# Attention output with the values stationary, two heads on two column halves, transposed by where it is written

## The chip, the cores and the metric

The kernel runs on one core of one Trainium2 chip. A core has five engines that work at the same time and wait for each other through semaphores: TensorE (matrix products, PE in the profile; its weight loads are PEld), VectorE (DVE), ScalarE (ACT), GpSimd (POOL) and SyncE (SP, whose queue issues most DMAs here). TensorE reads SBUF and writes PSUM; VectorE and ScalarE bring results from PSUM to SBUF. The metric is the device time of one execution in microseconds. All data are fp32.

## What is computed

The first part is a gated linear recurrence for 4 batches and 8 heads over 768 steps with head size 48. The second part is a layer with an oscillating activation on the 3072 x 384 result.

```python
for t in range(S):                                   # S = 768
    new_re = ar * S_re - ai * S_im                   # complex gate a[t], kept below magnitude 0.999
    new_im = ar * S_im + ai * S_re
    kv = np.einsum('bhd,bhe->bhde', k[:, :, t], v[:, :, t])
    S_re, S_im = (new_re + kv, new_im)
    y[:, :, t] = np.einsum('bhd,bhde->bhe', q[:, :, t], S_re)
...
x = y.transpose(0, 2, 1, 3).reshape(B * S, H * D)    # 3072 x 384
h = x @ w_in                                         # 384 x 2048
out = (h * np.cos(h)) @ w_out                        # 2048 x 384
```

## The kernel before

The kernel has a path for ordinary inputs (`fast_path`) and a general one that is taken only if a flag says that the products of gates have become too small; the profiled inputs take the first.

**Tiling.** Time is cut into chunks of C = 128 steps, 6 for each batch, N = 24 in all. G = 2 chunks make a group, so there are NG = 12 groups. The recurrence is turned into matrix products per chunk: the queries and the keys of each head are multiplied by running products of gates and stacked (real and imaginary part, 2 x 48 = 96 rows), so that the chunk's output is a masked 128 x 128 matrix of scores times the chunk's values, plus the queries times a 96 x 48 state that comes from the chunks before.

**Stages of a group**, and the lines that matter here:

- gates (`g_log`, `g_prod`, `g_angle`, `g_phase`, `g_trig`, `g_stack`): ScalarE, VectorE and GpSimd work out logarithms, angles and running products; TensorE sums over time with triangular matrices (`lgs` L662, `phs` L697 and L700).
- chunks, for each of the two chunks: `f_transpose` (TensorE transposes the keys and queries of four heads at a time into `tp`, L734, ScalarE copies them to `kT` and `qT`, L736); `f_scores` (`sc`, L744, masked by VectorE into `atm`, L746, which holds for each head the scores transposed, keys on the partitions and queries along the free dimension); `f_state` (`sp`, L769, the new state by VectorE and GpSimd, not for the last chunk of a batch); `f_out`; `f_xt`.
- `f_out` (L749 to L761): for each head, the scores `atm` are the stationary operand and the 48 columns of the values move (L755); where a state exists, the queries `qT` are stationary and the state's 48 columns move (L758), added in PSUM. The result `yp` has the 128 steps on the partitions and 8 x 48 columns. One ScalarE copy brings it to the SBUF tile `x` (L761). There is no state for the first chunk of a batch.
- `f_xt` (L782 to L789): the layer needs `x` with its 384 columns on the partitions, so TensorE transposes three blocks of 128 x 128 into `xp` (L788) and ScalarE copies them to `xT` (L789), a tile with 3 blocks for the two chunks of a group.
- `mm1` (L791 to L808), eight times a group: 2 x 3 products with blocks of `w_in` stationary and 256 moving columns of `xT` (`hp`, L796), then ScalarE (L802, and the sine at L619), VectorE (L803, L805, L807) make the gate.
- `mm2` (L810 to L817), twice a group: 16 products into `op` (L813), a ScalarE copy to `ot` (L816) and the store, issued on SP's queue (L817).

**Order.** The loop at L851 runs over `it`; at each `it` the gates of group `it`, the chunks of group `it - 1`, the `mm1` of group `it - 2` and the `mm2` of group `it - 3` are in work. `mm2` is written first, and the rest is interleaved by position (`weave`, L841). [...] `load` (L541) brings `re`, `im`, `k`, `q`, `v` by DMAs on SP's queue; the load of `v` for the group after the next is written behind the chunks of a group (L838). The weights are loaded and converted from 64-bit floats in the first pass of the loop.

PSUM has two rings of buffers: `pa` (5) for everything but the layer, `pm` (3) for `hp` and `op`. The pool `ft` holds two buffers of each of its tiles.

Of the kernel before, what the change touches and what calls it, by code (L numbers as in the profile page):

```python
# [11 lines left out]
F32 = mybir.dt.float32  # L12
# [473 lines left out]
def fast_path(ctx, tc, q, k, v, a_re, a_im, moe_w_in, moe_w_out, out, least):  # L486
# [4 lines left out]
    nc = tc.nc  # L491
    B, H, S, D = q.shape
    DM, DF = moe_w_in.shape
    C = 128
    NCH = S // C
    G = 2
# [3 lines left out]
    HH = H // 2  # L500
    ND = DM // C
# [7 lines left out]
    ft = ctx.enter_context(tc.tile_pool(name="ft", bufs=2))  # L509
    msb = ctx.enter_context(tc.tile_pool(name="msb", bufs=2))  # L510
    stage = ctx.enter_context(tc.tile_pool(name="stage", bufs=2))
    rows_d = ctx.enter_context(tc.tile_pool(name="rows_d", bufs=2, space=bass.MemoryType.DRAM))
    pa = ctx.enter_context(tc.tile_pool(name="pa", bufs=5, space=PSUM))
# [7 lines left out]
    def constant(array, name):  # L521
        t = consts.tile(list(array.shape), F32, name=name)
        nc.scalar.dma_start(out=t, in_=nc.inline_tensor(array, name=name + "_const").ap())
        return t
# [6 lines left out]
    X = [dict() for _ in range(NG)]  # L531
    Y = [dict() for _ in range(N)]

    def load(g, names):
        for name in names:
            ap = {"re": a_re, "im": a_im, "q": q, "k": k, "v": v}[name]
            X[g][name] = ld.tile([C, G, H, D], F32, tag=name, name=name,
                                 bufs=2 if name == "v" else 1)
            for i in range(G):
                b, c = divmod(g * G + i, NCH)  # L540
                nc.sync.dma_start(  # L541
                    out=X[g][name][:, i],
                    in_=ap[b].rearrange("h (c p) d -> p c h d", p=C)[:, c])
# [3 lines left out]
    ident = constant(np.eye(C, dtype=np.float32), "ident")  # L547
# [27 lines left out]
    def from_double(dst, src):  # L575
# [24 lines left out]
        nc.vector.scalar_tensor_tensor(out=dst, in0=e, scalar=897.0, in1=dst,  # L600
                                       op0=ALU.is_ge, op1=ALU.mult)

    chained = []

    def chain(ins):
# [121 lines left out]
    def f_transpose(n, name, hh):  # L727
        g, i = divmod(n, G)
        if hh == 0:
            Y[n][name] = ft.tile([D2, H, C], F32, tag=name, name=name)  # L730
        ps = pa.tile([D2, HH, C], F32, tag="a", name="tp")
        for h in range(HH):
            head = i * H + hh * HH + h
            nc.tensor.transpose(ps[:, h], X[g][name[0] + "s"][:, head].rearrange(  # L734
                "p a d -> p (a d)"), ident)
        nc.scalar.copy(out=Y[n][name][:, ts(hh, HH)], in_=ps)  # L736

    def f_scores(n, hh):
        y = Y[n]
        if hh == 0:  # L740
            y["atm"] = ft.tile([C, H, C], F32, tag="atm", name="atm")
        ps = pa.tile([C, HH, C], F32, tag="a", name="sc")
        for h in range(HH):
            nc.tensor.matmul(ps[:, h], lhsT=y["kT"][:, hh * HH + h], rhs=y["qT"][:, hh * HH + h],  # L744
                             start=True, stop=True)
        nc.vector.tensor_tensor(out=y["atm"][:, ts(hh, HH)], in0=ps,  # L746
                                in1=causal.unsqueeze(1).to_broadcast([C, HH, C]), op=ALU.mult)

    def f_out(n):  # L749
        y, (g, i) = Y[n], divmod(n, G)  # L750
        vals = X[g]["v"][:, i]
        state = y.get("state")
        ps = pa.tile([C, H, D], F32, tag="a", name="yp")
        for h in range(H):
            nc.tensor.matmul(ps[:, h], lhsT=y["atm"][:, h], rhs=vals[:, h],  # L755
                             start=True, stop=(state is None))
            if state is not None:
                nc.tensor.matmul(ps[:, h], lhsT=y["qT"][:, h], rhs=state[:, h],  # L758
                                 start=False, stop=True)
        y["x"] = ft.tile([C, DM], F32, tag="x", name="x")  # L760
        nc.scalar.copy(out=y["x"], in_=ps.rearrange("p h d -> p (h d)"))  # L761

    def f_state(n):
        if n % NCH == NCH - 1:
            return
        y, (g, i) = Y[n], divmod(n, G)
        ps = pa.tile([D2, H, D], F32, tag="a", name="sp")
        for h in range(H):
            nc.tensor.matmul(ps[:, h], lhsT=X[g]["ks"][:, i * H + h].rearrange("p a d -> p (a d)"),  # L769
                             rhs=X[g]["v"][:, i, h], start=True, stop=True)  # L770
        new = ft.tile([D2, H, D], F32, tag="state", name="state")
        end = X[g]["end"][:, ts(i, H)].unsqueeze(2).to_broadcast([D2, H, D])
        if "state" in y:
            nc.vector.scalar_tensor_tensor(out=new, in0=ps, scalar=0.25, in1=y["state"],  # L774
                                           op0=ALU.mult, op1=ALU.add)
            nc.gpsimd.tensor_tensor(out=new, in0=new, in1=end, op=ALU.mult)  # L776
        else:
            nc.vector.scalar_tensor_tensor(out=new, in0=ps, scalar=0.25, in1=end,
                                           op0=ALU.mult, op1=ALU.mult)
        Y[n + 1]["state"] = new  # L780

    def f_xt(n):  # L782
        g, i = divmod(n, G)
        if i == 0:
            X[g]["xT"] = msb.tile([C, ND, G, C], F32, tag="xT", name="xT")
        ps = pa.tile([C, ND, C], F32, tag="a", name="xp")
        for dc in range(ND):
            nc.tensor.transpose(ps[:, dc], Y[n]["x"][:, ts(dc, C)], ident)  # L788
        nc.scalar.copy(out=X[g]["xT"][:, :, i], in_=ps)  # L789

    def mm1(g, jp):  # L791
        x = X[g]
# [34 lines left out]
    def chunks(g):  # L827
        ns = range(g * G, g * G + G)
        for n in ns:
            for name in ("kT", "qT"):  # L830
                for hh in range(2):
                    yield lambda n=n, name=name, hh=hh: f_transpose(n, name, hh)
            for hh in range(2):
                yield lambda n=n, hh=hh: f_scores(n, hh)
            yield lambda n=n: f_state(n)
            yield lambda n=n: f_out(n)
            yield lambda n=n: f_xt(n)
        if g + 2 < NG:  # L838
            yield lambda: load(g + 2, ("v",))

# [10 lines left out]
    for it in range(NG + 3):  # L851
        g, c, m, o = it, it - 1, it - 2, it - 3
        if it == 0 and NG > 1:
            load(1, ("v",))
        if g < NG:
            g_log(g)
            g_prod(g)
            g_angle(g)
            if g + 1 < NG:
                load(g + 1, ("re", "im"))  # L860
        if it == 0:
            weave((gates(0), 0.0, 1.0), (weights, 0.2, 1.0))
            continue
        if 0 <= o < NG:
            for i in range(G):
                mm2(o, i)
        weave((gates(g) if g < NG else (), 0.0, 0.5),
              (chunks(c) if 0 <= c < NG else (), 0.0, 1.0),
              ([lambda jp=jp: mm1(m, jp) for jp in range(NJ // 2)] if 0 <= m < NG else (),
               0.0, 1.0))  # L870


@with_exitstack
def kernel(ctx, tc, q, k, v, a_re, a_im, moe_w_in, moe_w_out, out):

    nc = tc.nc
    D2, H = 2 * q.shape[3], q.shape[1]
    keep = ctx.enter_context(tc.tile_pool(name="keep", bufs=1))  # L880
    least = keep.tile([D2, 2 * H], F32, name="least")
    fast_path(tc, q, k, v, a_re, a_im, moe_w_in, moe_w_out, out, least)
    low = keep.tile([D2, 1], F32, name="low")
    nc.vector.tensor_reduce(out=low, in_=least, axis=AX.X, op=ALU.min)
    scratch = ctx.enter_context(tc.tile_pool(name="scratch", bufs=1,
                                             space=bass.MemoryType.DRAM))
    line_d = scratch.tile([D2], F32, name="line_d")
    nc.sync.dma_start(out=line_d, in_=low.rearrange("p o -> (p o)"))
    line = keep.tile([1, D2], F32, name="line")
    nc.sync.dma_start(out=line, in_=line_d.unsqueeze(0))  # L890
    bad = keep.tile([1, 2], F32, name="bad")
    nc.vector.tensor_reduce(out=bad[:, 0:1], in_=line, axis=AX.X, op=ALU.min)
    flag = keep.tile([1, 1], I32, name="flag")
    nc.vector.tensor_scalar(out=flag, in0=bad[:, 0:1], scalar1=0.5, scalar2=None, op0=ALU.is_lt)
    taken = nc.values_load(flag[0:1, 0:1], min_val=0, max_val=1,
                           skip_runtime_bounds_check_because="a comparison gives 0 or 1")
    with tc.If(taken > 0):
        general_path(tc, q, k, v, a_re, a_im, moe_w_in, moe_w_out, out)
# [30 lines left out]
```

## Time and profile before

| | us |
|---|---|
| median of 3 runs | 931.01 |
| lowest and highest | 930.38, 933.06 |
| the profiled execution | 938.23 |
| its span, first to last instruction | 936.4 |

Busy time by engine over the span is TensorE 797.1 us, VectorE 497.1, ScalarE 378.6, GpSimd 171.3. The largest groups of matmuls:

```profile
L796 PE MATMUL hp<-xT,w_in 128*128 128x256 f32 x1152 | 294.0, 409 | 4.1 <-DVE gate L807 3.5
L813 PE MATMUL op<-w_out,gate 128*128 128x384 f32 x768 | 251.1, 486 | 0.0
L744 PE MATMUL sc<-qT,kT 96*128 96x128 f32 x384 | 48.4, 277 | 0.1
```

How to read such a row: line, engine, operation, the tile written and the tiles read; then `128*128`, the rows and columns of the stationary operand, and `128x256`, the partitions and columns of the moving one; the count; then busy time in all and the mean duration in ns of one instruction; then the engine's idle time ahead of them and who ended it. Durations of matmuls overlap each other, so that the time a run of them takes is read from start to start, not by adding durations. Windows name a stretch of the span, its length, the busy time of an engine with its number of instructions, and the clock that TensorE was granted as a share of full speed.

### The profile page before, as it was taken

The page shows a single profiled execution, that of the slowest core. Times are in us where ns is not written, and L with a number is a line of the kernel's source. Part 1 is how long each engine was busy: PE and PEld are TensorE (multiplying, and loading weights), DVE is VectorE, ACT ScalarE, POOL GpSimd, SP SyncE. Part 2 cuts the span into 40 slices and gives each one's busy share as a digit, 9 for nine tenths or more (in the row PEclk, how much of TensorE's full clock was granted, in tenths as well). Part 3 has the DMA queues.
Part 4 walks back from the last instruction along what each step waited for, and adds up shares of the span by engine and source line. Part 5 has one row for each costly group of instructions (what it writes and reads, how often), then busy time and mean ns, then how long its engine had stood idle before and what let it go on. Part 6 is the DMA issues. An engine that isn't in the chain of part 4 may idle for free.

```text
span 936.4 us, 10169 instructions
## 1 busy us (share of the span) xinstructions
PE 797.1 (85%) x3920; PEld 621.0 (66%) x3920; DVE 497.1 (53%) x761; ACT 378.6 (40%) x588; POOL 171.3 (18%) x96
## 2 busy tenths in 40 slices
PE   1101446899999999999999999999999989999997
PEld 0000245685885977967968858858769668778684
DVE  3999985844544736636545446346456445123160
ACT  5222123535454554454364454354544623123140
POOL 2343333403103022112120031031030211000000
PEclk9999966899899999989899999898999998998999
DMA  8523631303004004004023040040040100000000
GB/s 174 141 90 112 146 108 34 69 18 63 23 18 85 1 18 85 1 17 85 1 43 60 18 83 3 18 85 1 18 84 1 26 10 1 9 9 1 9 8 21
DMA packets 151876, 42.03 MB, mean 45 GB/s; under 512 B 144638, under 2 KB 148222, under 8 KB 151818
## 3 DMA queue, kind: packets, MB, share of 16 engines
q1 hardware_dynamic: 151218, 40.98, 19.8%
q8 instruction: 33, 0.54, 0.3%
q10 hardware_dynamic: 600, 0.30, 0.1%
q14 instruction: 25, 0.20, 0.1%
HBM read 36.51 MB, written 4.76 MB: 44 GB/s over the span
## 4 chain that ended last, share of the span: by engine, by line
PE 70%; ACT 6%; DVE 2%; POOL 2%; DMA 1%; issue 1%; ACTq 0%; SPq 0%; POOLq 0%; DVEq 0%
PE hp L796 28%; PE op L813 17%; PE yp L755 4%; PE sc L744 4%; PE yp L758 4%; PE tp L734 4%; PE sp L769 3%; POOL m L646 2%; ACT rs L619 2%; PE lgs L662 1%; ACT L618 1%; PE phs L697 1%; PE phs L700 1%; PE xp L788 1%; ACT m L619 1%; ACT mag L619 1%
## 5 line engine op out<-in xcount | busy, mean ns | idle before, releaser
L796 PE MATMUL hp<-xT,w_in 128*128 128x256 f32 x1152 | 294.0, 409 | 4.1 <-DVE gate L807 3.5
L796 PEld LDWEIGHTS hp<-xT,w_in 128*128 128x128 f32 x1152 | 231.0, 207 | 39.7 <-DVE gate L807 3.9
L813 PE MATMUL op<-w_out,gate 128*128 128x384 f32 x768 | 251.1, 486 | 0.0
L813 PEld LDWEIGHTS op<-w_out,gate 128*128 128x128 f32 x768 | 145.9, 190 | 99.2
L803 DVE TENSOR_SCALAR cs<-turn 128x512 f32<-128x512 f32 x96 | 42.4, 443 | 172.9 <-ACT turn L802 172.9
L802 ACT ACTIVATE turn<-hp,quarter_b 128x512 f32<-128x512 f32 x96 | 65.7, 685 | 124.6 <-PE hp L796 122.7
L807 DVE TENSOR_TENSOR gate<-hp,cs 128x512 f32<-128x512 f32 x96 | 66.2, 690 | 82.2 <-ACT cs L619 81.4
L776 POOL TENSOR_TENSOR state<-state,end 96x384 f32<-96x384 f32 x16 | 31.2, 1949 | 342.2 <-DVE state L774 179.1
L755 PE MATMUL yp<-v,atm 128*128 128x48 f32 x384 | 75.3, 292 | 19.3 <-DVE atm L746 19.3
L619 ACT ACTIVATE cs<-cs 128x512 f32<-128x512 f32 x96 | 60.5, 630 | 69.0 <-DVE cs L805 69.0
L662 PE MATMUL lgs<-m,sums 128*128 128x384 f32 x48 | 21.3, 572 | 64.6 <-POOL m L646 49.3
L755 PEld LDWEIGHTS yp<-v,atm 128*128 128x128 f32 x384 | 62.0, 209 | 20.4 <-DVE atm L746 20.2
L758 PE MATMUL yp<-state,qT 96*128 96x48 f32 x320 | 67.7, 296 | 0.0
L805 DVE TENSOR_TENSOR cs<-turn,cs 128x512 f32<-128x512 f32 x96 | 65.9, 687 | 2.1
L662 PEld LDWEIGHTS lgs<-m,sums 128*128 128x128 f32 x48 | 9.2, 211 | 75.2 <-POOL m L646 71.3
L646 POOL TENSOR_TENSOR m<-m,rs 128x768 f32<-128x768 f32 x12 | 22.0, 1835 | 197.6 <-ACT rs L619 196.7
L697 PE MATMUL phs<-sq,sums 128*128 128x384 f32 x48 | 22.4, 557 | 38.8 <-DVE sq L688 38.8
L758 PEld LDWEIGHTS yp<-state,qT 96*128 96x128 f32 x320 | 54.2, 212 | 0.0
L761 ACT COPY x<-yp 128x384 f32<-128x384 f32 x24 | 11.5, 478 | 104.6 <-PE yp L758 94.0
L633 ACT ACTIVATE m<-re 128x768 f32<-128x768 f32 x12 | 10.1, 842 | 97.3 <-DMA re<-in_a_re_dram 97.3
L744 PE MATMUL sc<-qT,kT 96*128 96x128 f32 x384 | 48.4, 277 | 0.1
L744 PEld LDWEIGHTS sc<-qT,kT 96*128 96x128 f32 x384 | 46.9, 192 | 2.3 <-ACT qT L736 1.0
(77 smaller groups left out, 955.0 us busy)
## 6 DMA issues: line engine op xcount, KB each, us to landing
raw<-in_moe_w_in_dram SPq DMA_DIRECT2D x12, 512.0 KB
raw<-in_moe_w_out_dram SPq DMA_DIRECT2D x16, 384.0 KB
re<-in_a_re_dram SPq DMA_DIRECT2D x24, 192.0 KB
im<-in_a_im_dram SPq DMA_DIRECT2D x24, 192.0 KB
k<-in_k_dram SPq DMA_DIRECT2D x24, 192.0 KB
q<-in_q_dram SPq DMA_DIRECT2D x24, 192.0 KB
v<-in_v_dram SPq DMA_DIRECT2D x24, 192.0 KB
out_dram<-ot SPq DMA_DIRECT2D x24, 192.0 KB
```

The costliest lines, as they stand in the source:

```text
L619: chain(nc.scalar.activation(func=func, **kw))
L646: nc.gpsimd.tensor_tensor(out=m2, in0=m2, in1=rs, op=ALU.subtract)
L662: nc.tensor.matmul(ps, lhsT=sums, rhs=x["lg"][:, ts(i, DM)], start=True, stop=True)
L744: nc.tensor.matmul(ps[:, h], lhsT=y["kT"][:, hh * HH + h], rhs=y["qT"][:, hh * HH + h], start=True, stop=True)
L755: nc.tensor.matmul(ps[:, h], lhsT=y["atm"][:, h], rhs=vals[:, h], start=True, stop=(state is None))
L758: nc.tensor.matmul(ps[:, h], lhsT=y["qT"][:, h], rhs=state[:, h], start=False, stop=True)
L796: nc.tensor.matmul(ps[:, ji], lhsT=w_in[:, dc, ts(jp * 2 + ji, C)], rhs=x["xT"][:, dc].rearrange("p g t -> p (g t)"), start=(dc == 0), sto ...
L802: nc.scalar.activation(out=turn, in_=ps, func=AF.Identity, scale=INV_TWO_PI, bias=quarter_b)
L803: nc.vector.tensor_scalar(out=cs, in0=turn, scalar1=ROUND, scalar2=ROUND, op0=ALU.add, op1=ALU.subtract)
L805: nc.vector.tensor_tensor(out=cs, in0=turn, in1=cs, op=ALU.subtract)
L807: nc.vector.tensor_tensor(out=gate, in0=ps, in1=cs, op=ALU.mult)
L813: nc.tensor.matmul(ps, lhsT=X[g]["gate"][j // 2][:, j % 2, ts(i, C)], rhs=w_out[:, j], start=(j == 0), stop=(j == NJ - 1))
```

## The change

The output of a chunk is computed with the operands exchanged. For each head the 48 columns of the values are stationary and the 128 columns of `atm` move; then the state's 48 columns are stationary and the queries' 128 columns move. What comes out has the head's 48 dimensions on the partitions and the 128 steps along the free dimension: it is already transposed. Heads go in pairs: the even head of a pair is written to partitions 0 to 47 of PSUM, the odd one to partitions 64 to 111, and the pair `p` to columns block `p`. In each pair the order is: values of the even head, values of the odd head, state of the even head, state of the odd head. [...]

Two ScalarE copies per chunk (48 partitions x 512 each, one for each half) bring `yp` to a new tile `yT`, one buffer, which holds both chunks of a group. `f_xt` runs once a group instead of once a chunk. It has no transposes and no copy: DMAs on SP's queue bring the rows of each head from `yT` to their place in `xT`. The 48 rows of a head lie in one block of 128 or in two, so there are 10 DMAs a group, of 48, 32 or 16 partitions with 256 contiguous floats in each. The tile `x` goes. `queries` and the named `keys` in `f_state` change nothing in what is executed.

```diff
     def f_out(n):
         y, (g, i) = Y[n], divmod(n, G)
         vals = X[g]["v"][:, i]
         state = y.get("state")
-        ps = pa.tile([C, H, D], F32, tag="a", name="yp")
-        for h in range(H):
-            nc.tensor.matmul(ps[:, h], lhsT=y["atm"][:, h], rhs=vals[:, h],
-                             start=True, stop=(state is None))
+        if i == 0:
+            X[g]["yT"] = ft.tile([C, HH, G, C], F32, tag="yT", name="yT", bufs=1)
+        ps = pa.tile([C, HH, C], F32, tag="a", name="yp")
+        for p in range(HH):
+            for side in range(2):
+                nc.tensor.matmul(ps[ds(side * 64, D), p], lhsT=vals[:, 2 * p + side],
+                                 rhs=y["atm"][:, 2 * p + side], start=True, stop=(state is None))
             if state is not None:
-                nc.tensor.matmul(ps[:, h], lhsT=y["qT"][:, h], rhs=state[:, h],
-                                 start=False, stop=True)
-        y["x"] = ft.tile([C, DM], F32, tag="x", name="x")
-        nc.scalar.copy(out=y["x"], in_=ps.rearrange("p h d -> p (h d)"))
+                for side in range(2):
+                    nc.tensor.matmul(ps[ds(side * 64, D), p], lhsT=state[:, 2 * p + side],
+                                     rhs=queries(y, 2 * p + side), start=False, stop=True)
+        for side in range(2):
+            half = ds(side * 64, D)
+            nc.scalar.copy(out=X[g]["yT"][half, :, i], in_=ps[half])
...
-    def f_xt(n):
-        g, i = divmod(n, G)
-        if i == 0:
-            X[g]["xT"] = msb.tile([C, ND, G, C], F32, tag="xT", name="xT")
-        ps = pa.tile([C, ND, C], F32, tag="a", name="xp")
-        for dc in range(ND):
-            nc.tensor.transpose(ps[:, dc], Y[n]["x"][:, ts(dc, C)], ident)
-        nc.scalar.copy(out=X[g]["xT"][:, :, i], in_=ps)
+    def f_xt(g):
+
+        xt = X[g]["xT"] = msb.tile([C, ND, G, C], F32, tag="xT", name="xT")
+        for h in range(H):
+            row = h * D
+            while row < (h + 1) * D:
+                n = min((h + 1) * D, (row // C + 1) * C) - row
+                nc.sync.dma_start(out=xt[ds(row % C, n), row // C],
+                                  in_=X[g]["yT"][ds(h % 2 * 64 + row - h * D, n), h // 2])
+                row += n
...
             yield lambda n=n: f_state(n)
             yield lambda n=n: f_out(n)
-            yield lambda n=n: f_xt(n)
+            if n == ns[-1]:
+                yield lambda: f_xt(g)
```

More of the change, by code (lines that the diff above doesn't have):

```diff
@@ L736, in f_transpose, with queries @@
         nc.scalar.copy(out=Y[n][name][:, ts(hh, HH)], in_=ps)
+    def queries(y, h):
+        return y["qT"][:, h]
     def f_scores(n, hh):
@@ L743, in f_scores @@
         for h in range(HH):
-            nc.tensor.matmul(ps[:, h], lhsT=y["kT"][:, hh * HH + h], rhs=y["qT"][:, hh * HH + h],
+            nc.tensor.matmul(ps[:, h], lhsT=y["kT"][:, hh * HH + h], rhs=queries(y, hh * HH + h),
                              start=True, stop=True)
@@ L768, in f_state @@
         for h in range(H):
-            nc.tensor.matmul(ps[:, h], lhsT=X[g]["ks"][:, i * H + h].rearrange("p a d -> p (a d)"),
-                             rhs=X[g]["v"][:, i, h], start=True, stop=True)
+            keys = X[g]["ks"][:, i * H + h].rearrange("p a d -> p (a d)")
+            nc.tensor.matmul(ps[:, h], lhsT=keys, rhs=X[g]["v"][:, i, h], start=True, stop=True)
         new = ft.tile([D2, H, D], F32, tag="state", name="state")
```

## The prediction

> **What bounds the kernel now.** I read the page first (busy times, the clock line, the chain that ended last), then windows over single periods of the main loop, then the timeline of TensorE.
>
> ```profile
> PE 797.1 (85%) x3920; PEld 621.0 (66%) x3920; DVE 497.1 (53%) x761; ACT 378.6 (40%) x588; POOL 171.3 (18%) x96
> PE 70%; ACT 6%; DVE 2%; POOL 2%; DMA 1%; issue 1%; ACTq 0%; SPq 0%; POOLq 0%; DVEq 0%
> ```
>
> TensorE is busy 85% of the span of 936.4 us and holds 70% of the chain; no other engine passes 53%. The view of windows cuts the loop from one `lgs` matmul to the next, which is one group of two chunks (columns: stretch, its length, PE busy and instructions, granted clock, DMA share, GB/s):
>
> ```profile
> 284.54:348.79 64.25, 63.05 (x323) 0.97 0.19 38
> 482.14:544.70 62.56, 61.37 (x323) 1.00 0.20 39
> 199.60:868.40 668.80, 655.55 (x3315) 0.95 0.15 31
> ```
>
> In each period TensorE idles 1.2 us. The two single periods hold the same 323 instructions; the one granted 0.97 of the clock is 1.69 us longer. So in this stretch the time follows TensorE one for one, and TensorE's clock too. Over the 668.8 us from 199.6 to 868.4 the clock averages 0.95. Where it goes is in the timeline of TensorE (start, duration, line, operation, count):
>
> ```profile
> 567.86 1.95 PE L744 MATMUL sc<-qT,kT 96*128 96x128 f32 x16
> 569.64 2.75 PE L796 MATMUL hp<-xT,w_in 128*128 128x256 f32 x12
> 572.24 1.48 PE L769 MATMUL sp<-v,ks 128*96 128x48 f32 x16
> 573.55 0.39 PE L755 MATMUL yp<-v,atm 128*128 128x48 f32 x2
> 573.78 0.39 PE L758 MATMUL yp<-state,qT 96*128 96x48 f32 x2
> ...
> 577.25 4.38 PE L796 MATMUL hp<-xT,w_in 128*128 128x256 f32 x12
> 581.47 0.49 PE L788 MATMUL xp<-ident,x 128*128 128x128 f32 x3
> 581.79 1.04 PE L734 MATMUL tp<-ident,ks 128*96 128x128 f32 x8
> 582.67 2.76 PE L796 MATMUL hp<-xT,w_in 128*128 128x256 f32 x12
> ```
>
> Pitch is read from start to start. Twelve `hp` of 256 moving columns take 2.60 us (569.64 to 572.24), 217 ns each; sixteen `sc` of 128 columns take 1.78, 111 ns each: 0.85 ns a column. But `yp` moves only 48 columns, 41 ns worth, and still needs 112 ns (0.23 to 0.22 us for two, 32 in 3.6 us), and `sp`, also 48 columns, 82 ns (1.31 for 16). 112 to 82 is the ratio of their stationary widths, 128 to 96: these two are held by the weight load, and the array streams 36% and 50% of their time. Right behind them the same twelve `hp` take 4.38 instead of 2.76 us: the clock has halved. Eleven such dips lie between 199.6 and 868.4, the first and last of the view of windows and its sum over all eleven being
>
> ```profile
> 204.96:208.60 3.64, 3.64 (x12) 0.54 0.57 108
> ...
> 843.80:850.60 6.80, 6.80 (x24) 0.54 0.00 1
> sum 59.24, PE 59.24; mean PE 5.39
> ```
>
> All eleven begin inside a `yp` run or at its end, with TensorE busy in its rows. They come only where `sp` and a full `yp` stand together (1.3 + 3.6 = 4.9 us of thin streaming). Behind the shorter stretch of a batch's first chunk (no state, 3.1 us) the clock stays:
>
> ```profile
> 512.00:520.00 8.00, 8.00 (x52) 1.00 0.00 1
> ```
>
> 59.24 us at about half clock are 29 us lost. That the dips are caused by thin streaming is my reading of where they begin; the trace doesn't name a cause.
>
> [...]
>
> **The change part by part.** *The products.* The groups by form:
>
> ```profile
> L755 PE MATMUL yp<-v,atm 128*128 128x48 f32 x384 | 75.3, 292 | 19.3 <-DVE atm L746 19.3
> L758 PE MATMUL yp<-state,qT 96*128 96x48 f32 x320 | 67.7, 296 | 0.0
> L788 PE MATMUL xp<-ident,x 128*128 128x128 f32 x72 | 14.4, 318 | 1.1 <-ACT x L761 1.1
> L761 ACT COPY x<-yp 128x384 f32<-128x384 f32 x24 | 11.5, 478 | 104.6 <-PE yp L758 94.0 <-PE yp L755 10.6
> L789 ACT COPY xT<-xp 128x384 f32<-128x384 f32 x24 | 11.4, 474 | 7.7 <-PE xp L788 7.7
> L736 ACT COPY qT<-tp 96x512 f32<-96x512 f32 x48 | 27.0, 582 | 0.7 <-PE tp L734 0.5
> ```
>
> An fp32 product is two matmul rows (24 chunks x 8 heads = 192 products, 384 rows), and the count stays at 704. Each now holds 48 columns stationary and moves 128: 111 ns by the `sc` row, with a weight load of about 41 ns hidden under it (an estimate from the 82 and 112 ns). Taken singly nothing is won. The even head writes output partitions 0 to 47, the odd one 64 to 111, so the two use separate column halves of the array. No row shows two matmuls at once. Bounds per chunk with state (32 rows): wholly serial, 32 x 0.112 = 3.58 us as now; overlapped, the second row of one half beside the first of the other half, 17 slots of 0.112 = 1.90 us. I take the overlap, since the sides share no stationary columns and no output partitions, and program order alternates them after every product. Entering and leaving the split array may empty the pipeline: a pair of rows lasts 0.39 us while the next starts 0.22 later, a tail of 0.166. Bounds 0 and two tails a chunk; I take two, 0.33 us. So 2.23 us a chunk, 1.35 won; a chunk without state 9 x 0.112 + 0.33 = 1.34 for 1.79, 0.45 won. From chunk 2 on there are 19 and 3 of them: 25.7 + 1.3 = **27 us**.
>
> [...]
>
> *The clock.* The new `yp` streams 128 columns in every slot, so the thin stretch shrinks to `sp`'s 1.3 us, below the 3.1 us that left the clock whole. All eleven dips go: **29 us** (bounds 0 and 29).
>
> *The transposes.* Three `xp` rows take 0.33 us from 581.47 to 581.79 (x72 in all); 22 chunks give **7 us**. The waits for `x` were 1.1 us, nothing.
>
> *ScalarE.* Two copies go (478 and 474 ns), two of 48x512 come; the row of the same 512 elements a partition has 582. That is 0.21 us more a chunk, 5 us in all, behind TensorE: the 94.0 us of idle time before L761 hide it. Uncovered it would cost those 5. Can ScalarE and VectorE follow a faster TensorE? At the end `hp` runs alone and they keep its pace of 2.6 us:
>
> ```profile
> 888.92 20.88 PE L796 MATMUL hp<-xT,w_in 128*128 128x256 f32 x96
> ```
>
> *The ten DMAs a group.* Eight heads, two of them cut at a 128 boundary: 10 DMAs of 16 to 48 partitions, 1 KB a partition, from SP's queue. What stands there now, and the cover on TensorE, in the timeline:
>
> ```profile
> 598.28 0.99 SPq L541 DMA_DIRECT2D v<-in_v_dram  x2
> ...
> 617.83 0.99 SPq L541 DMA_DIRECT2D im<-in_a_im_dram  x2
> 619.21 0.36 SPq L817 DMA_DIRECT2D out_dram<-ot  x1
> ...
> 868.28 20.81 PE L813 MATMUL op<-w_out,gate 128*128 128x384 f32 x64
> ```
>
> and, from the chain and from the waits of SP's queue (us in total, times, longest):
>
> ```profile
> 749.85 2.27 DMA end<-row
> ```
>
> ```profile
> SPq L541 <- PE yp L758: 235.0, 7, 36.6
> ```
>
> Ten issues at 0.36 to 0.5 us (L817, L541) are 3.6 to 5 us. SP's queue waits for the last copy into `yT`; behind it stands only the load of `v` for a group used two periods later, which waits for the same `yp` already (issued at 598.28). SP's next issue is at 617.83.
>
> From the end of `yp`: copies 1.2, issue 5, landing 2.3 (the 48-partition `end` load): 8.5 us. `hp`, which waited for ScalarE's copy of `xT`, now waits for DMAs, but it comes only after the 64 `op` rows of the next period, 20.8 us of TensorE. Hidden, with 12 us to spare; POOL's queue isn't touched. The one `yT` buffer is read out long before the next group's first copy, some 30 us later. The first group has no `op` in front:
>
> ```profile
> 146.91 0.66 PE L755 MATMUL yp<-v,atm 128*128 128x48 f32 x2 [7.14 <-DVE atm L746]
> ...
> 156.01 6.38 PE L796 MATMUL hp<-xT,w_in 128*128 128x256 f32 x18 [0.57 <-ACT xT L789]
> ```
>
> There 8.5 us stand for about 2.3 from the end of `yp` (153.7) to `hp`, 6 us more, against about 3 from the half-clock `yp` ahead of it and the transposes; the gates and their waits around it make it uncertain. I count 0 (bounds -3 and +3).
>
> **Sum:** 27 + 29 + 7 = 63 us. Against the profiled span, 936.4 - 63 = 873. The runs have a median of 931.01, 5 us below that span; the same 63 us give **868**.
>
> **The rivals.**
> *No overlap* (the fp32 pairs run one after the other; for it: no row shows two matmuls at once; against it: separate halves). The products win nothing and pay 7 us of tails; transposes and clock stay won: 931 + 7 - 7 - 29 = 902.
> *Dips stay*, with overlap (half an array in use might count as thin, or the cause is another): 931 - 27 - 7 = 897. Against it: where the clock fell, in all eleven.
> *Neither*: 931 + 7 - 7 = 931, no change.
> *Every change of half empties the pipeline.* `f_out` alternates halves after each product, 16 times a chunk with state and 8 without: 19 x 16 + 3 x 8 = 328 changes of 0.166 us, 54 us. With the clock won this gives 931 + 54 - 29 - 7 = **949, slower**. It decides the sign from (29 + 7) / 328 = 0.11 us a change on. For it: the tail exists in every row. Against it: between lines of unlike shapes (`sp` to `yp`, `tp` to `hp`) no such gap is seen.
>
> **How the numbers follow.** Overlap and clock 0.53, no overlap 0.18, dips stay 0.11, neither 0.05, emptied pipeline 0.13. The first three reach from 860 (no tails: 7 us less) with 5 us more for the loop's own waits, 855, up to 902 with the startup and ScalarE terms uncovered, 910; that holds 0.82. A difference of 0.3%, 3 us, is about what a measurement of this kernel can tell from no change: faster 0.82, same 0.05, slower 0.13.
>
> **What would show it.** Overlap: `yp` at 56 ns a row from start to start, a full chunk's `yp` in about 2.2 us. No overlap: 112 ns and 3.9 us. An emptied pipeline: over 0.2 us between the last row of one half and the first of the other. Clock: 1.00 in the windows from 200 to 868. DMAs: `hp` waiting for a DMA into `xT` in more than the first period would prove me wrong there; so would a ScalarE that `hp` waits for. The forecast falls if the rows of the two halves don't overlap, or if dips follow `yp` again.

## The result and the profile after

| | before | after |
|---|---|---|
| median, us | 932.03 (4 runs) | 868.16 (4 runs) |
| lowest and highest, us | 930.38, 935.01 | 866.92, 869.62 |
| span of the profiled execution, us | 936.4 | 867.7 |

The ratio is 0.9312, with a 95% interval from 0.928 to 0.9344: faster by 6.9%. The forecast was 868.

The page of the changed kernel, its busy times and the chain that ended last, in the order of the lines shown of before:

```profile
PE 723.2 (83%) x3848; PEld 546.0 (63%) x3848; DVE 496.8 (57%) x761; ACT 387.8 (45%) x588; POOL 158.5 (18%) x96
PE 68%; DVE 12%; ACT 8%; POOL 5%; issue 3%; DMA 2%; SPq 0%; ACTq 0%; POOLq 0%
```

TensorE lost 74 us of busy time and still holds most of the chain; ScalarE gained 9. The 72 instructions that are gone are the transposes. The groups of the products and of the copies:

```profile
L762 PE MATMUL yp<-atm,v 128*48 128x128 f32 x384 | 37.7, 285 | 17.7 <-DVE atm L750 17.7
L766 PE MATMUL yp<-qT,state 96*48 96x128 f32 x320 | 32.2, 279 | 0.0
L770 ACT COPY yT<-yp 48x512 f32<-48x512 f32 x48 | 27.7, 577 | 41.2 <-PE yp L766 33.5 <-PE yp L762 7.2
```

As many rows as before, 384 and 320, of nearly the same length each (285 for 292 ns), are busy for 70 us instead of 143: rows lie beside each other. The windows, columns as before (the period has the same place in a batch as the two quoted of before, but fewer instructions, since its transposes are gone):

```profile
450.12:510.08 59.96, 58.77 (x316) 1.00 0.23 47
200.00:864.00 664.00, 646.21 (x3424) 1.00 0.18 39
```

The clock is 1.00 from 200 to 864 us, and the period takes 59.96 us where the undisturbed one of before took 62.56. The timeline of TensorE around one chunk with state:

```profile
433.11 2.75 PE L807 MATMUL hp<-xT,w_in 128*128 128x256 f32 x12
435.80 0.43 PE L762 MATMUL yp<-atm,v 128*48 128x128 f32 x4
436.05 0.39 PE L766 MATMUL yp<-qT,state 96*48 96x128 f32 x4
...
437.37 0.39 PE L766 MATMUL yp<-qT,state 96*48 96x128 f32 x4
437.69 2.86 PE L807 MATMUL hp<-xT,w_in 128*128 128x256 f32 x12
```

Four rows go in 0.22 us, 55 ns a row, where two did. The `hp` ahead ends its pitch at 433.11 + 2.60 = 435.71, the first `yp` starts 0.09 us later, and behind the last four rows (437.37 + 0.22) there are another 0.10 us. From 435.71 to 437.69 the chunk's `yp` takes 1.98 us; in an undisturbed chunk of before it was 3.58:

```profile
528.39 0.39 PE L755 MATMUL yp<-v,atm 128*128 128x48 f32 x2
...
531.97 1.09 PE L796 MATMUL hp<-xT,w_in 128*128 128x256 f32 x4
```

**Where the span's difference lies.** Cut at the `lgs` that opens the first full period and at the 64 `op` that follow the last chunk (before 218.90 and 868.28; after 211.67 and 797.96), the stretch of chunks 4 to 23 went from 649.38 to 586.29 us, 63.1 less, and the start gave 7.2; behind the cut the changed kernel is 1.6 longer (69.7 for 68.1 us). In the stretch: 17 chunks with state at 1.60 and three without at about 0.68 give 29, and twenty times three transposes at 0.33 give 6.6. The dips were more than the prediction counted. Its windows cut several of them short, and there is a twelfth, which follows no `yp` but a wait of TensorE:

```profile
764.46 1.44 PE L700 MATMUL phs<-ph,last 128*128 128x384 f32 x2 [2.50 <-DVE ph L704]
```

```profile
764.72:768.13 3.41, 3.41 (x8) 0.50 0.00 0
```

At their full lengths in the trace, four of 3.41 us and seven of 6.83 (the last of these from 843.22 to 850.05), the eleven dips behind 218.9 are 61.45 us at a clock of 0.50, about 30.7 lost: 29 in the ten that follow `yp` and 1.7 in this one. That makes 66.5, 3.4 more than the stretch lost. The rest is visible in the undisturbed period: it lost 2.60 us (62.56 to 59.96), where one chunk with state, one without and six transposes give 2.94, so other rows of TensorE take 0.34 us more, and ten times that is 3.4. In that period it is `sc` (32 rows take 3.76 us from start to start, 3.57 before) and `hp`; why was not tried.

The wait for `ph` stands at the same place in every kernel here, 2.50 to 3.44 us long. A dip of 3.41 us follows it in five traces (before, and of the kernels below the side-major order, the half changing after two heads, the transposes put back and the doubled DMAs) and not in the other five. Four of the five kernels with it move 128 columns, and the length of the wait does not decide it either: 2.50 us in the kernel before had a dip, 3.44 in the first kernel below had none. So up to 1.7 us of a difference between two kernels below can come from there.

### The profile page after: what moved, and what is told of

Same layout as the page of the kernel before. It is cut to its first block, busy times and chain, and to the rows that moved or that the text cites. A ratio compares the mean times of both kernels' runs of the same rounds, so it can differ in the third digit from the quotient of the medians.

```text
span 867.7 us, 10233 instructions
## 1 busy us (share of the span) xinstructions
PE 723.2 (83%) x3848; PEld 546.0 (63%) x3848; DVE 496.8 (57%) x761; ACT 387.8 (45%) x588; POOL 158.5 (18%) x96
## 4 chain that ended last, share of the span: by engine, by line
PE 68%; DVE 12%; ACT 8%; POOL 5%; issue 3%; DMA 2%; SPq 0%; ACTq 0%; POOLq 0%
PE hp L807 28%; PE op L824 18%; PE sc L748 5%; PE tp L735 4%; PE sp L779 3%; PE yp L762 3%; POOL m L647 2%; PE lgs L663 2%; ACT rs L620 2%; PE yp L766 2%; POOL w_out L596 2%; ACT L619 1%; PE phs L698 1%; PE phs L701 1%; ACT m L620 1%
## 5 line engine op out<-in xcount | busy, mean ns | idle before, releaser
L807 PE MATMUL hp<-xT,w_in 128*128 128x256 f32 x1152 | 266.9, 382 | 3.9 <-DMA xT<-yT 3.9
L807 PEld LDWEIGHTS hp<-xT,w_in 128*128 128x128 f32 x1152 | 213.8, 190 | 38.4 <-issue 7.3
L785 POOL TENSOR_TENSOR state<-state,end 96x384 f32<-96x384 f32 x16 | 17.8, 1109 | 319.4 <-DVE state L783 161.3
L762 PE MATMUL yp<-atm,v 128*48 128x128 f32 x384 | 37.7, 285 | 17.7 <-DVE atm L750 17.7
L748 PE MATMUL sc<-qT,kT 96*128 96x128 f32 x384 | 50.6, 283 | 0.1
L770 ACT COPY yT<-yp 48x512 f32<-48x512 f32 x48 | 27.7, 577 | 41.2 <-PE yp L766 33.5
L827 ACT COPY ot<-op 128x384 f32<-128x384 f32 x24 | 11.2, 466 | 60.4 <-PE op L824 60.4
L650 DVE SCALAR_TENSOR_TENSOR sq<-mag,sq 128x768 f32<-128x768 f32 x12 | 12.6, 1047 | 43.7 <-POOL mag L649 43.7
L719 POOL TENSOR_TENSOR Q<-k,Q 128x768 f32<-128x768 f32 x12 | 26.9, 2239 | 55.0 <-DMA row<-P 34.6
```

Of the source, the lines that this page charges most:

```text
L762: nc.tensor.matmul(ps[ds(side * 64, D), p], lhsT=vals[:, 2 * p + side], rhs=y["atm"][:, 2 * p + side], start=True, stop=(state is None))
L807: nc.tensor.matmul(ps[:, ji], lhsT=w_in[:, dc, ts(jp * 2 + ji, C)], rhs=x["xT"][:, dc].rearrange("p g t -> p (g t)"), start=(dc == 0), sto ...
```

## The experiments

The theory is the prediction's: two halves at work at once, a clock that no longer falls because the products stream in every slot, and transposes that TensorE no longer makes. Each is tried by itself. Each kernel below was timed beside the kernel before on the same chip; before had a median of 933.47 us beside the wide, the side-major, the head-major and the transposes' kernel, and of 933.68 beside the other four. Ratios are to it.

**The clock alone.** The kernel before, with 128 columns moving in place of 48 and the same stationary operands. The extra columns belong to other heads, and the heads overwrite each other in a `yp` of four blocks of 128, so this kernel's output is not the attention output:

```diff
...
-            nc.tensor.matmul(ps[:, h], lhsT=y["atm"][:, h], rhs=vals[:, h],
+            at = ds(min(h * D, DM - C), C)
+            nc.tensor.matmul(ps[:, h % HH], lhsT=y["atm"][:, h], rhs=wide[:, at],
...
-                nc.tensor.matmul(ps[:, h], lhsT=y["qT"][:, h], rhs=state[:, h],
+                nc.tensor.matmul(ps[:, h % HH], lhsT=y["qT"][:, h], rhs=held[:, at],
...
```

> The kernel before with one thing changed: 128 columns of the values and of the state move in each product of yp instead of 48 (the extra columns belong to other heads, heads overwrite each other in PSUM, so x holds other numbers). The weight loads stay, so the pitch stays at 0.112 us. If thin streaming causes the dips, the clock is 1.00 from 200 to 868 us and the time falls by what the dips cost, 24 to 29 us: 903 to 908 us. Rival (dips come from the weight loads or from the length of the run): 932 us, clock 0.95 in that stretch.

904.26 us, ratio 0.9693 (0.9668 to 0.9718): 29 us less, with more arithmetic. The timeline of this kernel around a chunk, and its window over the stretch:

```profile
556.22 0.45 PE L758 MATMUL yp<-v,atm 128*128 128x128 f32 x2
556.50 0.39 PE L761 MATMUL yp<-state,qT 96*128 96x128 f32 x2
...
559.86 0.38 PE L799 MATMUL hp<-xT,w_in 128*128 128x256 f32 x1
```

```profile
200.00:833.00 633.00, 618.82 (x3269) 1.00 0.16 33
```

The run of 32 rows takes as long as before (556.22 to 559.86, 3.64 us, with 3.58 before), its weight loads have the same shape and length (a median of 0.19 us, as before), and the clock is 1.00 from 200 to 833 us. So it was neither the length of the run nor the weight loads: with 128 columns moving in place of 48 the dips that follow `yp` are gone, where the kernel before had a clock of 0.95 from 199.6 to 868.4. By what the clock comes to follow the width, no run shows. That the layer works on other numbers here is not the reason either: the side-major kernel below computes the right ones and has no dip behind `yp`. The stretch between the two cuts takes 620.21 us here (213.23 to 833.44), 29.2 less than in the kernel before; the dip behind the wait for `ph`, which is missing here, is 1.7 of that.

**The overlap alone.** The changed kernel, all even heads first (values, then state of each), then all odd ones:

```diff
-        for p in range(HH):
-            for side in range(2):
+        for side in range(2):
+            for p in range(HH):
                 nc.tensor.matmul(ps[ds(side * 64, D), p], lhsT=vals[:, 2 * p + side],
...
```

> The changed kernel with the same products in another order: all of the even heads first (one column half), then all of the odd heads. If the gain of the products comes from two halves at work at once, and a row overlaps only with a neighbour in program order, only one handover per chunk is left: 31 slots of 0.112 us and two gaps of 0.1 instead of 1.98 us, 3.67 us a chunk with state, 1.69 more, and 0.75 more without: 19 x 1.69 + 3 x 0.75 = 34 us, 902 us. If the clock's dips come from thin streaming, the clock stays at 1.00 from 200 us on, since 128 columns move in each slot. Rival (dips come from the length of sp and yp together, 5 us again): dips return, 27 us more, 929 us. Rival (halves don't matter): 868 us.

899.3 us, ratio 0.9634 (0.9607 to 0.966): 31 us of the gain are gone, with the same instructions in another order. No dip follows a `yp` run (the clock is 1.00 from 200 to 890 us, and the one dip of the stretch, at 736.80, follows the wait for `ph`), so the rival that the dips come from length falls here too. The timeline of one chunk:

```profile
430.75 0.42 PE L762 MATMUL yp<-atm,v 128*48 128x128 f32 x2
...
431.89 0.38 PE L765 MATMUL yp<-qT,state 96*48 96x128 f32 x2
432.11 0.42 PE L762 MATMUL yp<-atm,v 128*48 128x128 f32 x4
432.33 0.42 PE L765 MATMUL yp<-qT,state 96*48 96x128 f32 x4
432.59 0.38 PE L762 MATMUL yp<-atm,v 128*48 128x128 f32 x2
...
434.00 2.86 PE L806 MATMUL hp<-xT,w_in 128*128 128x256 f32 x12
```

The rows go by twos, one half at work, up to the one place where the half changes: there four and four go together. The run takes 3.25 us, about 28 slots behind a 0.1 us gap, where I had expected 31. At that place rows of the second half start beside the last four of the first (eight rows in 0.48 us, from 432.11 to 432.59, where eight of one half take 0.88, from 431.01 to 431.89), although they come behind them in the program. I had assumed that only direct neighbours overlap. The list of TensorE's instructions in the compiled program keeps the order of kernel.py (values and state of the last even head, then values and state of the first odd one), while four `yp<-atm,v` start in a row here, from 432.11, and four `yp<-qT,state` behind them, from 432.33: the starts do not stand in the order of that list. By what, no trace shows.

**How far ahead?** Two more orders: the half changes after each head (4 rows with state), and after two heads (8 rows).

```diff
         for p in range(HH):
             for side in range(2):
                 nc.tensor.matmul(ps[ds(side * 64, D), p], lhsT=vals[:, 2 * p + side],
                                  rhs=y["atm"][:, 2 * p + side], start=True, stop=(state is None))
-            if state is not None:
-                for side in range(2):
+                if state is not None:
                     nc.tensor.matmul(ps[ds(side * 64, D), p], lhsT=state[:, 2 * p + side],
...
```

> The changed kernel with values and state of one head in a row, then the other head: the half changes after four rows instead of two. If rows overlap only where the half changes in program order, a chunk with state has 7 handovers and 25 slots of 0.112 us: 3.0 instead of 1.98 us, 1.0 more, none more without a state: 19 us, 887 us. Rival (the queue looks ahead far enough to pair rows of the two halves in any order): 868 us. Rival (no overlap at all in this order): 902 us.

869.21 us, ratio 0.9318 (0.9291 to 0.9345): the same as the changed kernel, whose interval it shares nearly end for end. 32 rows stand in 1.92 us, by the window over one chunk of it, counting `yp` alone; the second fence is the same window in the changed kernel:

```profile
434.40:436.40 2.00, 1.92 (x32) 1.00 0.00 0
```

```profile
435.70:437.70 2.00, 1.91 (x32) 1.00 0.00 0
```

```diff
-        for p in range(HH):
+        for pp in range(2):
             for side in range(2):
+                for p in range(2 * pp, 2 * pp + 2):
...
```

> The changed kernel with the half changing after two heads (8 rows with state) instead of one (4) or one product (2). If TensorE can start a row of the other half about 4 or 5 rows ahead of its turn, as the one handover of the side-major order showed, a chunk with state takes 19 to 20 slots, 0.25 us more than 17, and one without a state as much: 5 us, 873 us. Rival (rows start in program order and the head-major order had another reason): 29 slots, 1.3 us more, 25 us, 893 us. Rival (any depth): 868 us.

882.14 us, ratio 0.9453 (0.9409 to 0.9496), 14 more than the changed kernel where I had expected 5. The window over one chunk, and its timeline from the first handover to the start of the second:

```profile
441.30:443.80 2.50, 2.46 (x32) 1.00 0.00 0
```

```profile
441.81 0.42 PE L763 MATMUL yp<-atm,v 128*48 128x128 f32 x4
442.04 0.43 PE L766 MATMUL yp<-qT,state 96*48 96x128 f32 x4
442.30 0.42 PE L763 MATMUL yp<-atm,v 128*48 128x128 f32 x4
```

2.46 us with one gap are about 21 slots. Each of the three handovers pairs four rows of one half with four of the other, as the single one did, and takes 0.48 to 0.49 us where four slots are 0.44. So in both orders a handover paired about four rows and no more. My figure was too low because it took 19 to 20 slots against 17: the changed kernel takes 16, and four slots with three times 0.04 us are 0.56 us a chunk with state and not 0.25. In this kernel the stretch between the cuts is 11.8 us longer (213.85 to 811.97, 598.1 us), up to 1.7 of it a dip at 722.60 behind the wait for `ph`, and the start 2.2.

**The transposes alone.** The changed kernel with three transposes and a copy per chunk put back, their result unused:

```diff
             nc.scalar.copy(out=X[g]["yT"][half, :, i], in_=ps[half])
+        xp = pa.tile([C, ND, C], F32, tag="a", name="xp")
+        for dc in range(ND):
+            nc.tensor.transpose(xp[:, dc], y["atm"][:, dc], ident)
+        spare = ft.tile([C, ND, C], mybir.dt.bfloat16, tag="spare", name="spare", bufs=1)
+        nc.scalar.copy(out=spare, in_=xp)
```

> The changed kernel with three transposes and one ScalarE copy of 384 elements a partition added back in each chunk (of atm, the result unused). If TensorE sets the pace, 22 x 0.33 = 7 us more: 875 us. Rival (they fit into gaps of TensorE): 868 us.

875.78 us, ratio 0.9388 (0.9361 to 0.9415): 7.6 us more. From the first `xp` to the `hp` behind it there are 0.38 us in its timeline:

```profile
438.65 0.55 PE L773 MATMUL xp<-ident,atm 128*128 128x128 f32 x3
439.03 2.76 PE L812 MATMUL hp<-xT,w_in 128*128 128x256 f32 x12
```

A period without a dip takes 60.53 us (451.36 to 511.89) where the changed kernel's takes 59.96: 0.57 us for six transposes. The stretch between the cuts is 7.1 us longer (210.66 to 804.07, 593.4 us), ten times 0.57 and a dip at 715.56 behind the wait for `ph`. So TensorE sets the pace here, and the transposes do not fit into gaps; their own price is nearer to 6 us than to 7.6.

**What I had counted at nothing.** ScalarE's copies and SP's DMAs, each doubled in a kernel of its own; the extra copies go to an unused tile, the extra DMAs to unused DRAM:

```diff
...
         for side in range(2):
             half = ds(side * 64, D)
+            nc.scalar.copy(out=spare[half], in_=ps[half])
             nc.scalar.copy(out=X[g]["yT"][half, :, i], in_=ps[half])
```

> The changed kernel with each copy of yp made twice (the extra ones into an unused bf16 tile, ahead of the needed ones): 48 more ScalarE copies of about 0.58 us, 28 us of ScalarE work, 1.2 us later for yT in each chunk. If ScalarE lies behind TensorE, within 2 us of 868. Rival (the copies stand on the path, and the bank of yp or the turn behind them is late): 24 x 0.6 to 1.2, 882 to 896 us.

```diff
...
-                nc.sync.dma_start(out=xt[ds(row % C, n), row // C],
-                                  in_=X[g]["yT"][ds(h % 2 * 64 + row - h * D, n), h // 2])
+                for t in (spare, xt):
+                    nc.sync.dma_start(out=t[ds(row % C, n), row // C],
+                                      in_=X[g]["yT"][ds(h % 2 * 64 + row - h * D, n), h // 2])
```

> The changed kernel with each of the ten DMAs of a group issued twice (the extra ones to an unused DRAM tile): 120 more issues of 0.36 to 0.6 us on SP's queue, 5 us a group. If the 20.8 us of op cover them, only the first group pays: 5 to 6 us more in its wait for xT, part of it inside other waits of the start, 869 to 874 us. Rival (SP's queue or the landing is on the path of each group): 12 x 5 us, 928 us.

870.03 us, ratio 0.9331 (0.9289 to 0.9374), and 869.5 us, ratio 0.932 (0.9278 to 0.9362). Both intervals hold the changed kernel's 0.9312: twice the copies and twice the DMAs cost nothing that these runs can tell, and far less than the rivals' 14 and 60 us. In the changed kernel one group's DMAs stand so on SP's queue, and TensorE's next `hp` so:

```profile
439.05 6.66 SPq L798 DMA_DIRECT2D xT<-yT  x10
445.76 0.58 SPq L541 DMA_DIRECT2D v<-in_v_dram  x1
...
465.50 2.75 PE L807 MATMUL hp<-xT,w_in 128*128 128x256 f32 x12
```

Ten issues end 8.1 us behind the end of `yp` at 437.6, and `hp` comes 19.8 us behind them. Only the first group has no such cover; among TensorE's waits in the changed kernel is

```profile
PE hp L807 <- DMA xT<-yT: 3.9, 1, 3.9
```

**A version that tries to win that wait.** The first group's DMAs on two queues:

```diff
-                nc.sync.dma_start(out=xt[ds(row % C, n), row // C],
+                queue = nc.scalar if g == 0 and h % 2 else nc.sync
+                queue.dma_start(out=xt[ds(row % C, n), row // C],
...
```

> The changed kernel with the first group's DMAs of odd heads on ScalarE's queue, the others on SP's. If the wait of 3.9 us for xT before the first hp is the issue of ten DMAs one after the other (6.3 us) and TensorE's start follows from it, half of it goes: 865 to 867 us. Rival (the gates of the next group set the start, or ScalarE's issues delay them): 868 to 870 us.

871.55 us, ratio 0.9344 (0.9302 to 0.9386): no gain, and 1.6 us more than even the rival's 868 to 870. TensorE's waits and timeline in this kernel:

```profile
PE hp L808 <- DMA xT<-yT: 3.5, 1, 3.5
```

```profile
154.74 5.38 PE L808 MATMUL hp<-xT,w_in 128*128 128x256 f32 x10 [3.55 <-DMA xT<-yT]
160.81 1.56 PE L663 MATMUL lgs<-m,sums 128*128 128x384 f32 x4 [0.69 <-POOL m L647]
```

`hp` starts at 154.74 as in the changed kernel, and the order of the start came out otherwise: ten `hp` instead of four stand ahead of `lgs`, which starts at 160.81 instead of 158.18. The next `lgs` is 2.4 us late (214.10 for 211.67). What bounds the start was not settled; no version here beats the changed kernel.

## Why the prediction was right

| term | predicted, us | measured, us |
|---|---|---|
| products on two halves | 27 | 29 in 20 chunks by the trace; 28.5 from 904.26 to 875.78, with all else that those two kernels differ in |
| clock | 29 | 29 (933.47 to 904.26), 29.2 in the stretch of the trace, 1.7 of it the dip behind the wait |
| transposes | 7 | 7.6 (875.78 to 868.16, each in its own set of runs); by the traces about 6 and a dip |
| copies, DMAs | 0 | within the noise when doubled |
| start | 0 | 7.2, of which about 6 are chunks 2 and 3 and one dip, which the predicted terms above include |
| sum of the span | 63 | 68.7 |
| sum of the runs | 63 | 64 |

*Bound.* TensorE set the pace from 200 us on: three added transposes per chunk came back as 0.57 us a period, and the same instructions in an order that leaves one half idle as 31.

*Overlap.* It came, at 55 ns a row. The 1.98 us of a chunk are two gaps of 0.09 and 0.10 us and 16 slots, where I took two tails of 0.166 and 17 slots. So a chunk won 1.60 and not 1.35, about 5 us over all chunks. The dips were about 3 us more than I had them, and 3.4 us were lost again in other rows; what else the start won, 1.5 us, the end lost. Together that is about the 5.7 us that the span won beyond 63. The reason that I gave for the overlap, program order alternating after every product, is not needed: alternating after each head gives the same time (869.21 us, and 868.16).

*Clock.* The cause stood for the eleven dips at `yp`: they go when 128 columns stream, with overlap (a clock of 1.00 from 200 to 864 us) or without (1.00 from 200 to 833 in the wide kernel). The twelfth I had missed; it follows a wait in kernels of either width, and that it is gone in the changed kernel's trace is luck, since half of the kernels here show it. In the 3.41 us ahead of each of the eleven, a stretch as long as the shorter dips, TensorE was busy throughout (from 573.57 to 576.98, say, 3.41 us in 33 rows). Only ahead of the twelfth was it idle, for 2.50 us.

*Rivals.* "No overlap" put 902 on the table, and the side-major order, which comes near to it, ran at 899.3. "Dips stay" and "neither" fall with the window at 1.00. "Every change of half empties the pipeline" falls with the four rows per 0.22 us across changes of half.

*DMAs.* `hp` waited for them in the first group alone, 3.9 us of the 6 that I had worked out against the shorter `yp`. Ten issues took 6.7 us, more than my 3.6 to 5, as a copy inside SBUF took 0.59 us to issue (the median of 120) and not 0.36 to 0.5; the cover was large enough.

*The runs.* That the median came out within 0.2 us of the forecast is partly chance: the profiled execution of before was 6 us above its median, and errors of 3 to 5 us in the terms stood against each other.

## What to carry to other kernels

Read matmuls from start to start and ask what holds the pitch: here 48 columns moved past a weight load of 128 at 0.112 us a row, and exchanging the operands left the pitch of a row as it was (0.11 us in the side-major kernel), gave room for two halves (55 ns a row) and gave the result in the layout that the next stage wants. Look at the granted clock behind each run of thin matmuls, for most of what they cost here stood in the rows behind them: between before and the wide kernel `hp` alone went from 231.4 to 207.4 us in the stretch, read from start to start, 24 of its 29. When the transposed layout costs small DMAs, look for what the consumer runs first: 20 us of other products hid ten DMAs, and ten more into DRAM.

## What was not expected of the hardware

A matmul of one column half started beside matmuls of the other half that stand ahead of it in the program: in the side-major kernel four rows were paired at the one place where the half changes (eight rows in 0.48 us), four at each of three such places in the order by twos (0.48 to 0.49 us each), and with a change after every four rows the 32 rows of a chunk stand in 1.92 us, with a change after two in 1.91. In the first three of these orders four `yp<-atm,v` start in a row where the program has two and then two `yp<-qT,state` (432.11 us in the side-major kernel, 441.81 in the order by twos), so here, for fp32 on two column halves, the starts were not held to the order of the program (the ends in a trace are modelled and show nothing of it). That the reach is about four rows is read from these four orders; a longer or shorter mix of rows was not tried.

Ahead of the first row on two halves there were 0.09 us and behind the last 0.10 (435.71 to 435.80 and 437.59 to 437.69 in the changed kernel), less than the tail of a row, 0.166 us by the prediction.
